# Attention scored two tiles at a time, and a 32 bytes longer mu tile, in a fused local-attention and channel-mix kernel

## The chip, the core and the metric

The kernel runs on one core of one Trainium2 chip. The metric is the device time of one execution in microseconds (us), over several runs; one more execution is recorded by the hardware profiler, and all views of the profile come from that one. The engines have these names: PE does the matmuls (its weight loads are shown apart, as PEld), DVE is the vector engine, ACT the scalar engine, POOL the GpSimd engine, and SP issues the DMAs.

## What is computed

Attention over a short window is followed by a gated channel mix. The inputs are float32; batch 4, 8 heads, 768 tokens, head dimension 64, so d_model is 512, and d_ff is 1024.

```
for each chunk of 32 queries:
    keys = 8 memory keys + 16 tokens to the left + the 32 of the chunk + 8 to the right   # 64
    a = softmax(q_c @ keys.T / 8);  out_c = a @ values
x = the heads of out put side by side                     # (4, 768, 512)
x_prev = x shifted by one token, zero at the start
xk = mu_k * x + (1 - mu_k) * x_prev;   xr = mu_r * x + (1 - mu_r) * x_prev
v = relu(xk @ w_k) ** 2 @ w_v;         r = sigmoid(xr @ w_r)
result = r * v
```

## The kernel before

**Tiles and units.** Tokens come in 24 tiles of 128 (`t`), and two neighbouring tiles make one of 12 units of 256 tokens (`u`). Attention is done by tile, the channel mix by unit.

**Attention of a tile** (`attention`). `f_load` brings queries and windows of keys, 1 MB, into a buffer with the tag `big` (three buffers, shared with the raw weights). The queries lie block-diagonal: a pair of heads shares the 128 partitions, with zeros off the diagonal, so that one matmul over 128 rows gives 64 rows of scores, 32 queries of either head. `f_s` (line 310) makes 16 such matmuls of 64 columns into the PSUM tile `s`. Each float32 matmul is two weight loads and two MATMUL instructions, so 16 of them are 32 MATMULs in the trace. Softmax follows: maximum on DVE (321), subtraction on DVE (325), exponential on ACT (333), sum, an added constant and a reciprocal on DVE (337 to 339), and the multiplication on DVE or POOL (343). `f_t` (349) transposes on PE into `pt`, `f_bd` copies `pt` into a zeroed block tile `aTz` in two halves (215 on ACT, 217 on DVE), `f_a` (368) multiplies by the values into `px`, and `f_x` copies into `xT`, which has one column more than the unit for the token before it.

**Preparation of a unit** (`prep`). `df` is the difference of neighbouring tokens (424), then for r and after it for k: four instructions of mix with mu (432), a rounded high part `xh`, and the remainder `xl` (442).

**Channel mix of a unit** (`channel_mix`). Everything is split into a high and a low part, and each product is three float32r matmuls. `f_gate` gives `pr` (461, 24 matmuls of 512 columns, into one PSUM tile of two banks), `f_sig` its sigmoid over both halves at once (479); `f_s1` gives `ph` (493, four blocks of 24 matmuls of 256 columns), then relu, square, high and low part as `kh` and `kl` (501 to 518); `f_s2` gives `pv` (549, 48 matmuls of 512 columns in four quarters), `f_o` multiplies by the gate (563), `f_st` stores (566).

**Weights.** Each of the ten 1 MB blocks (two of w_r, four of w_k, four of w_v) arrives as raw float64 words and is turned into a high and a low float32r tile by ACT and DVE: 257, 260, 264, then the high part (215 or 217) and the low part (270). All of that lies at the start of the kernel.

**The order.** The instructions are not ordered by a scheduler at run time. `te_order` writes out an order for PE and gives each entry a due time from `PE_COST`; `Plan.dues` passes due times backwards; `Plan.order` then places the operation that can start first by its own cost table, the earlier due time deciding a tie, and picks the engine where there is a choice (`either`). So every engine's queue is fixed when the kernel is built. A `Slot` stands for a buffer, and an operation that needs a new one must wait until the users of an older one are placed. Before the first `ph` block, gaps that the plan sees on PE are filled with `warm` matmuls on zeros (589), as many as fit by its own table. In the order before, t and a of a tile of unit u+2 come in unit u, one tile in the middle of `ph` and one in the middle of `pv`, and s of the next tile right behind a.

**Places in SBUF.** Tiles of the pool `const` are laid out in order of their declaration: identity, mu (32 bytes in each partition), the split weights, `aTz`, a zero tile; the work buffers follow.

Of the kernel before, what the change touches and what calls it, by code (L numbers as in the profile page):

```python
# [40 lines left out]
PE_COST = {"s": 1.05, "t": 0.45, "a": 1.05, "g": BLOCK, "h": BLOCK, "v": BLOCK}  # L41
# [94 lines left out]
def te_order():  # L136

    nu = B * S // UTOK
    seq = LEAD.split()
    seq = [tuple([x[0]] + [int(n) for n in x[1:].split(".")]) for x in seq]  # L140
    for u in range(nu):
        a, b = 2 * u + 4, 2 * u + 5
        g = [("g", u + 1, c) for c in range(QPU)] if u + 1 < nu else []
# [4 lines left out]
    nq = B * NQT  # L148
    seq = [x for x in seq if not (x[0] in "sta" and x[1] >= nq)]
# [9 lines left out]
def local_attention__then__channel_mix(  # L159
# [72 lines left out]
    o_mu = op(("dma", 0.1), lambda: nc.sync.dma_start(mu_sb, mu))  # L232
# [53 lines left out]
    xslot = {}  # L286

    def attention(t):
        b, i = qts[t]
        u, c = t // QPU, t % QPU  # L290

        def f_load():
            a = T["qk", t] = sb("big", [P, QKW], f"qk{t}")
            nc.sync.dma_start(a, qk[b, i])
# [5 lines left out]
        def f_s():  # L300
            s = T["s", t] = ps("s", f"s{t}")
            s4 = s.rearrange("p (m r k) -> p m r k", m=2, r=NPAIR)
            a = T["qk", t]
            nq = NPAIR * NJ * 2 * CHUNK
            q4 = a[:, :nq].rearrange("p (r j q) -> p r j q", r=NPAIR, j=NJ)
            k4 = a[:, nq:].rearrange("p (r j k) -> p r j k", r=NPAIR, j=NJ)
            for r in range(NPAIR):
                for j in range(NJ):
                    o = 64 * (j % 2)
                    nc.tensor.matmul(  # L310
                        s4[o : o + 64, j // 2, r, :], q4[:, r, j, :], k4[:, r, j, :], start=True, stop=True
                    )

        def f_max():
            s = T["s", t].rearrange("p (m r k) -> p m r k", m=2, r=NPAIR)
            if i == 0:
                nc.vector.memset(s[0:64, 0, :, 0:LEFT], NEG)
            if i == NQT - 1:
                nc.vector.memset(s[64:P, 1, :, LEFT + CHUNK : LEFT + CHUNK + RIGHT], NEG)
            mx = T["mx", t] = sb("sm", [P, 2 * NPAIR], f"mx{t}")  # L320
            nc.vector.reduce_max(mx, T["s", t].rearrange("p (g k) -> p g k", k=NK), axis=AX.X)  # L321

        def f_sub():
            e = T["e", t] = sb("e", [P, 2 * NPAIR, NK], f"e{t}")
            nc.vector.tensor_sub(  # L325
                e,
                T["s", t].rearrange("p (g k) -> p g k", k=NK),
                T["mx", t].unsqueeze(2).to_broadcast([P, 2 * NPAIR, NK]),
            )

        def f_exp():
            e = T["e", t]
            nc.scalar.activation(e, e, AF.Exp, scale=SCALE)  # L333

        def f_sum():
            sm = T["sum", t] = sb("sm", [P, 2 * NPAIR], f"sum{t}")
            nc.vector.reduce_sum(sm, T["e", t], axis=AX.X)
            nc.vector.tensor_scalar_add(sm, sm, 1e-9)
            nc.vector.reciprocal(sm, sm)  # L339

        def f_norm(g):
            e = T["e", t]
            g.tensor_mul(e, e, T["sum", t].unsqueeze(2).to_broadcast([P, 2 * NPAIR, NK]))  # L343

        def f_t():
            p = T["pt", t] = ps("tp", f"pt{t}")
            e = T["e", t].rearrange("p (n r) k -> p n (r k)", r=2)
            for n in range(4):
                nc.tensor.transpose(p[:, n * P : (n + 1) * P], e[:, n, :], id_sb)  # L349
# [8 lines left out]
        def f_a():  # L358
            a = aTz[t % bufs["aT"]].rearrange("p (m g c h) s q -> p m g c h (s q)", m=2, g=2, c=2)
# [3 lines left out]
            for m in range(2):  # L363
                for cc in range(2):
                    for g in range(2):
                        for h in range(2):
                            j = 2 * m + cc
                            nc.tensor.matmul(  # L368
                                p3[64 * h : 64 * h + 64, 2 * g : 2 * g + 2, CHUNK * j : CHUNK * j + CHUNK],
                                v[:, g, h, j, :],  # L370
                                a[:, m, g, cc, h, :],
                                start=True,
                                stop=True,
                            )

        def f_x(e):
            if c == 0:
                x = T["xT", u] = sb("xT", [P, KT, 1 + UTOK], f"xT{u}")
                if units[u][1] == 0:
                    nc.gpsimd.memset(x[:, :, 0:1], 0.0)  # L380
                else:
                    nc.gpsimd.tensor_copy(x[:, :, 0:1], T["xT", u - 1][:, :, UTOK : UTOK + 1])
# [6 lines left out]
        qs, vs, s1, s2, s3 = Slot("big"), Slot("vw"), Slot("s"), Slot("tp"), Slot("tp")  # L389
        m1, m2, e = Slot("sm"), Slot("sm"), Slot("e")  # L390
# [3 lines left out]
        ds, dt, da = (due[x, t] for x in "sta")  # L394
        l = op(("dma", 3.0), f_load, new=[qs])
        lv = op(("dma", 1.5), f_loadv, new=[vs])
        o_s = op(("pe", 1.05), f_s, [l, prior.get("s")], new=[s1], use=[qs], due=ds)
        o_m = op(("dve", 0.62), f_max, [o_s], new=[m1], use=[s1], due=ds + 3)
        o_b = op(("dve", 0.62), f_sub, [o_m], new=[e], use=[s1, m1], due=ds + 4)
        o_e = op(("act", 0.55), f_exp, [o_b], use=[e])  # L400
        o_u = op(("dve", 0.98), f_sum, [o_e], new=[m2], use=[e])
        o_n = op(either(dve=(0.62, True), pool=(1.0, True)), f_norm, [o_u], use=[e, m2])
# [4 lines left out]
        prior.update(s=o_s, t=o_t, a=o_a)  # L407
# [3 lines left out]
        xdone[t] = op(either(act=(0.5,), dve=(0.61,)), f_x, deps, new=[xslot[u]] if c == 0 else [], use=[s3, xslot[u]], due=da + 4)  # L411
# [38 lines left out]
    def channel_mix(u):  # L450
        b, t0 = units[u]

        def f_gate(c):
            if c == 0:
                T["pr", u] = ps("g", f"pr{u}", QPU)
            p = T["pr", u][:, c * DM : (c + 1) * DM]
            xh, xl = T["xh", u, 1], T["xl", u, 1]
            wh, wl = ([w[k // 2][:, k % 2 * DM : (k % 2 + 1) * DM] for k in range(KT)] for w in wr_hl)
            for k in range(KT):
                for n, (x, w) in enumerate(((xh, wh[k]), (xh, wl[k]), (xl, wh[k]))):  # L460
                    nc.tensor.matmul(  # L461
                        p, x[:, k, c * P : (c + 1) * P], w, start=(k + n == 0), stop=(k == KT - 1 and n == 2)
                    )

        gs = Slot("g")
        grp = []
        for c in range(QPU):
# [4 lines left out]
                    new=[gs] if c == 0 else [], use=list(mix[u, 1][2:]) + ([gs] if c else []),  # L472
                    due=due["g", u, c],
                )
            )

        def f_sig():
            g = T["sg", u] = sb("sg", [P, QPU * DM], f"sg{u}")
            nc.scalar.activation(g, T["pr", u], AF.Sigmoid)

        sgs = Slot("sg")
        o_g = op(("act", 0.48 * QPU + 2.6), f_sig, grp, new=[sgs], use=[gs], due=due["g", u, 1] + BLOCK + 4)
# [49 lines left out]
        for c in range(QPU):  # L532
# [36 lines left out]
            o_o = op(("dve", 0.62), f_o, [prev, o_g], new=[os], use=[s, sgs], due=dv + BLOCK + 2)  # L569
# [4 lines left out]
    for t in range(len(qts)):  # L574
        attention(t)
# [67 lines left out]
```

## Time and profile before

| what | us |
|---|---|
| median of 3 runs (lowest, highest) | 439.28 (439.17, 439.79) |
| the profiled execution, its own time | 439.1 |
| its span in the profile | 437.3 |
| PE busy, share of the span | 430.8, 99% |
| PE weight loads busy | 382.6, 88% |
| DVE busy | 257.8, 59% |
| ACT busy | 194.2, 44% |
| POOL busy | 26.4, 6% |
| moved by DMA | 55.15 MB |

A row of the groups view reads: line, engine, operation, output and inputs, shapes, number of instructions, then busy time in us and the mean of one in ns, then the idle time of the engine ahead of them with what ended it. The chain of waits is followed back from the last instruction, and each of its rows has a start, a length and what filled it. PE being busy for 99% of the span says little by itself, since the `warm` matmuls count as busy too, and since a matmul is counted from its start to its modelled end, so that neighbours overlap.

### The profile page before, as it was taken

How to read it: one execution, taken by the hardware profiler on the slowest of the kernel's cores; microseconds unless marked ns; L12 is line 12 of the kernel's file. 1: busy time of each engine (PE TensorE's matmuls, PEld its weight loads, DVE VectorE, ACT ScalarE, POOL GpSimd, SP SyncE). 2: the span in 40 equal slices, each digit the busy share in tenths (PEclk: the TensorE clock that was granted, in tenths of full speed). 3: DMA queues.
4: the chain of work that ended last, by engine and by line, in shares of the span. 5: the costliest groups of instructions: out<-in, count | busy, mean ns of one | idle time of the engine just before them, and what ended most of it. 6: DMA issues, size and time to landing. Idle time of an engine off the chain costs nothing.

```text
span 437.3 us, 8807 instructions
## 1 busy us (share of the span) xinstructions
PE 430.8 (99%) x3868; PEld 382.6 (88%) x3868; DVE 257.8 (59%) x426; ACT 194.2 (44%) x266; POOL 26.4 (6%) x33
## 2 busy tenths in 40 slices
PE   9999999989999999999999999999999999999996
PEld 8899988888898898898898898898898898798894
DVE  2899999973654745744844835835736737522121
ACT  1767595552353353264254354354354354152150
POOL 2100030100100100100100100100100010000000
PEclk9999999999999999999999999999999999999999
DMA  8988767621331431421512422413401200000101
GB/s 323 411 318 298 295 247 272 257 93 51 143 130 45 165 105 53 183 68 79 190 54 94 171 69 100 169 43 128 168 28 46 73 25 1 25 25 0 49 0 48
DMA packets 12901, 55.15 MB, mean 126 GB/s; under 512 B 1472, under 2 KB 1600, under 8 KB 9280
## 3 DMA queue, kind: packets, MB, share of 16 engines
q1 hardware_dynamic: 12864, 54.60, 33.8%
q8 instruction: 30, 0.49, 0.5%
q14 instruction: 7, 0.06, 0.0%
HBM read 48.30 MB, written 6.29 MB: 125 GB/s over the span
## 4 chain that ended last, share of the span: by engine, by line
PE 94%; DVE 3%; ACT 2%; issue 0%
PE ph L493 30%; PE pv L549 30%; PE pr L461 15%; PE px L368 6%; PE warm L589 6%; PE s L310 5%; PE pt L349 2%; ACT aTz L215 1%; DVE e L343 1%; DVE o L563 0%; DVE df L432 0%; DVE mx L321 0%; ACT L333 0%; DVE xl L442 0%; DVE mag L264 0%; DVE df L424 0%
## 5 line engine op out<-in xcount | busy, mean ns | idle before, releaser
L493 PE MATMUL ph<-xh,wkh 128*128 128x256 f32 x384 | 109.6, 285 | 0.0
L493 PE MATMUL ph<-xh,wkl 128*128 128x256 f32 x384 | 107.8, 281 | 0.0
L493 PE MATMUL ph<-xl,wkh 128*128 128x256 f32 x384 | 107.8, 281 | 0.0
L549 PE MATMUL pv<-wvh,kh 128*128 128x512 f32 x192 | 77.8, 405 | 0.0
L549 PE MATMUL pv<-wvh,kl 128*128 128x512 f32 x192 | 76.1, 396 | 0.0
L549 PE MATMUL pv<-wvl,kh 128*128 128x512 f32 x192 | 75.6, 394 | 0.0
L493 PEld LDWEIGHTS ph<-xh,wkh 128*128 128x128 f32 x384 | 72.3, 188 | 1.2
L493 PEld LDWEIGHTS ph<-xl,wkh 128*128 128x128 f32 x384 | 72.4, 188 | 0.5
L493 PEld LDWEIGHTS ph<-xh,wkl 128*128 128x128 f32 x384 | 72.4, 188 | 0.0
L518 DVE TENSOR_TENSOR kl<-kf,kh 128x512 fp32r<-128x512 f32 x45 | 31.1, 691 | 69.7 <-ACT kh L215 69.6
L501 ACT ACTIVATE kf<-ph 128x512 f32<-128x512 f32 x48 | 28.7, 598 | 80.5 <-PE ph L493 80.5
L549 PEld LDWEIGHTS pv<-wvh,kl 128*128 128x128 f32 x192 | 36.0, 188 | 8.7
L549 PEld LDWEIGHTS pv<-wvh,kh 128*128 128x128 f32 x192 | 36.1, 188 | 8.4
L549 PEld LDWEIGHTS pv<-wvl,kh 128*128 128x128 f32 x192 | 36.1, 188 | 7.9
L461 PE MATMUL pr<-wrh,xl 128*128 128x512 f32 x96 | 38.1, 397 | 0.0
L461 PE MATMUL pr<-wrh,xh 128*128 128x512 f32 x96 | 38.0, 396 | 0.0
L461 PE MATMUL pr<-wrl,xh 128*128 128x512 f32 x96 | 37.8, 394 | 0.0
L217 DVE COPY aTz<-pt 64x512 f32<-64x512 f32 x29 | 20.0, 690 | 26.4 <-PE pt L349 26.3
L343 POOL TENSOR_TENSOR e<-e,sum 128x512 f32<-128x512 f32 x10 | 16.7, 1667 | 261.0 <-DVE sum L339 261.0
L424 DVE TENSOR_TENSOR df<-xT 128x1024 f32<-128x1024 f32 x12 | 14.7, 1223 | 28.7 <-ACT xT L215 28.7
L333 ACT ACTIVATE e<-e 128x512 f32<-128x512 f32 x24 | 15.2, 632 | 36.3 <-DVE e L325 36.2
L508 ACT ACTIVATE kf<-kf 128x512 f32<-128x512 f32 x48 | 30.3, 631 | 1.2
(55 smaller groups left out, 576.2 us busy)
## 6 DMA issues: line engine op xcount, KB each, us to landing
qk<-in_qk_dram SPq DMA_DIRECT2D x24, 1024.0 KB, 7.4
vw<-in_vw_dram SPq DMA_DIRECT2D x24, 512.0 KB, 3.8
out_dram<-o SPq DMA_DIRECT2D x24, 256.0 KB, 2.0
raw<-in_w_k_dram SPq DMA_DIRECT2D x4, 1024.0 KB, 5.3
raw<-in_w_v_dram SPq DMA_DIRECT2D x4, 1024.0 KB, 8.0
raw<-in_w_r_dram SPq DMA_DIRECT2D x2, 1024.0 KB, 9.8
id_sb<-in_ident_dram SPq DMA_DIRECT2D x1, 64.0 KB, 8.9
mu_sb<-in_mu_dram SPq DMA_DIRECT2D x1, 4.0 KB, 9.4
```

What stands on the lines that cost most here:

```text
L217: e.tensor_copy(dst, src)
L310: nc.tensor.matmul(s4[o : o + 64, j // 2, r, :], q4[:, r, j, :], k4[:, r, j, :], start=True, stop=True)
L333: nc.scalar.activation(e, e, AF.Exp, scale=SCALE)
L343: g.tensor_mul(e, e, T["sum", t].unsqueeze(2).to_broadcast([P, 2 * NPAIR, NK]))
L368: nc.tensor.matmul(p3[64 * h : 64 * h + 64, 2 * g : 2 * g + 2, CHUNK * j : CHUNK * j + CHUNK], v[:, g, h, j, :], a[:, m, g, cc, h, :], sta ...
L461: nc.tensor.matmul(p, x[:, k, c * P : (c + 1) * P], w, start=(k + n == 0), stop=(k == KT - 1 and n == 2))
L493: nc.tensor.matmul(p[:, i * UTOK : (i + 1) * UTOK], w[:, fc], x[:, k], start=(k + n == 0), stop=(k == KT - 1 and n == 2),)
L501: e.activation(r, T["ph", u, f], AF.Relu)
L508: e.activation(q, q, AF.Square)
L518: e.tensor_sub(l, T["kf", u, f], T["kh", u, f].bitcast(F32))
L549: nc.tensor.matmul(p, x[:, tc_], w, start=(f + n == 0), stop=(f == FT - 1 and n == 2))
L589: nc.tensor.matmul(warm[:, :P], zero_sb, zero_sb, start=True, stop=True)
```

## The change

It has two parts.

- Attention goes by units. Queries are no longer block-diagonal: the two heads of a pair lie in partitions 0 to 63 and 64 to 127, and each is multiplied by itself, 64 rows by 32 columns, into a bank of its own. A load is 768 KB in place of 1 MB. The scores of a unit are 64 matmuls (`f_s` in the new `scores`) into one PSUM tile of two banks, and each step of softmax is one instruction over 1024 elements. `f_t`, `f_bd`, `f_a`, `f_x` stay by tile, with other index patterns. The token before a unit is copied on ACT in place of POOL. The gate has its PSUM in two buffers of the tag `m` with a sigmoid for each half. The buffer counts change: `big` 3 to 4, `x4` 5 to 4, `e` 2 to 1 (twice as large), `xT` 3 to 2, `m` 3 to 4, `g` gone, `s` twice as large. The written order changes: both tiles of unit u+1 (no longer of u+2) go through t after the second `ph` block of unit u and through a after the third, s of unit u+2 follows, and the gate of unit u+1 comes after the first quarter of `pv`.
- The tile of mu is declared with 64 bytes in each partition in place of 32, of which half is used, so that all tiles behind it lie 32 bytes further on.

```diff
-LEAD = "s0 t0 a0 s1 t1 a1 s2 t2 a2 s3 g0.0 g0.1 t3 a3 s4"
+LEAD = "s0 t0 t1 a0 a1 s1 g0.0 g0.1"
-QKW = NPAIR * NJ * (2 * CHUNK + NK)
+QKW = NPAIR * NJ * (CHUNK + NK)
-PE_COST = {"s": 1.05, "t": 0.45, "a": 1.05, "g": BLOCK, "h": BLOCK, "v": BLOCK}
+PE_COST = {"s": 1.9, "t": 0.45, "a": 1.05, "g": BLOCK, "h": BLOCK, "v": BLOCK}
...
-        seq += h[:2] + [("t", a)] + h[2:3] + [("a", a), ("s", b)] + h[3:] + g + [("t", b)]
-        seq += v[:1] + [("a", b), ("s", a + 2)] + v[1:]
+        seq += h[:2] + [("t", a), ("t", b)] + h[2:3] + [("a", a), ("a", b), ("s", u + 2)] + h[3:]
+        seq += v[:1] + g + v[1:]
...
-        "big": 3, "vw": 2, "x4": 5,
-        "e": 2, "sm": 2, "xT": 3, "kf": 2, "sg": 2, "o": 3,
-        "s": 1, "tp": 2, "g": 1, "m": 3, "aT": 2,
+        "big": 4, "vw": 2, "x4": 4,
+        "e": 1, "sm": 2, "xT": 2, "kf": 2, "sg": 2, "o": 3,
+        "s": 1, "tp": 2, "m": 4, "aT": 2,
...
-    mu_sb = const.tile([P, 2, KT], F32, tag="mu", name="mu_sb")
+    mu_sb = const.tile([P, 4, KT], F32, tag="mu", name="mu_sb")
...
+    def scores(u):
+        def f_s():
+            s = T["s", u] = ps("s", f"s{u}", QPU)
+            s5 = s.rearrange("p (h c r k) -> p h c r k", h=2, c=QPU, r=NPAIR)
...
+                for r in range(NPAIR):
+                    for j in range(NJ):
+                        for h in range(2):
+                            z = slice(64 * h, 64 * h + 64)
+                            nc.tensor.matmul(
+                                s5[CHUNK * j : CHUNK * (j + 1), h, c, r, :], q4[z, r, j, :], k4[z, r, j, :],
+                                start=True, stop=True,
+                            )
...
+        l = [op(("dma", 2.3), lambda t=t: f_load(t), new=[x]) for t, x in zip(ts, qs)]
+        o_s = op(("pe", 1.9), f_s, l + [prior.get("s")], new=[s1], use=qs, due=ds)
+        o_m = op(("dve", 1.15), f_max, [o_s], new=[m1], use=[s1], due=ds + 4)
+        o_b = op(("dve", 1.15), f_sub, [o_m], new=[e], use=[s1, m1], due=ds + 5.5)
+        o_e = op(("act", 1.0), f_exp, [o_b], use=[e])
+        o_u = op(("dve", 1.55), f_sum, [o_e], new=[m2], use=[e])
+        o_n = op(either(dve=(1.15, True), pool=(2.2, True)), f_norm, [o_u], use=[e, m2])
...
-            if c == 0:
-                T["pr", u] = ps("g", f"pr{u}", QPU)
-            p = T["pr", u][:, c * DM : (c + 1) * DM]
+            p = T["pr", u, c] = ps("m", f"pr{u}_{c}")
...
+        def f_sig(c):
+            if c == 0:
+                T["sg", u] = sb("sg", [P, QPU * DM], f"sg{u}")
+            nc.scalar.activation(T["sg", u][:, c * DM : (c + 1) * DM], T["pr", u, c], AF.Sigmoid)
```

More of the change, by code (lines that the diff above doesn't have):

```diff
@@ L141, in te_order @@
     for u in range(nu):
-        a, b = 2 * u + 4, 2 * u + 5
-        g = [("g", u + 1, c) for c in range(QPU)] if u + 1 < nu else []
+        a, b = 2 * u + 2, 2 * u + 3
+        g = [("g", u + 1, c) for c in range(QPU)]
         h = [("h", u, f) for f in range(FT // 2)]
         v = [("v", u, c, n) for c in range(QPU) for n in range(2)]
-        seq += h[:2] + [("t", a)] + h[2:3] + [("a", a), ("s", b)] + h[3:] + g + [("t", b)]
-        seq += v[:1] + [("a", b), ("s", a + 2)] + v[1:]
-    nq = B * NQT
-    seq = [x for x in seq if not (x[0] in "sta" and x[1] >= nq)]
+        seq += h[:2] + [("t", a), ("t", b)] + h[2:3] + [("a", a), ("a", b), ("s", u + 2)] + h[3:]
+        seq += v[:1] + g + v[1:]
+    last = {"s": nu, "g": nu, "t": B * NQT, "a": B * NQT}
+    seq = [x for x in seq if x[1] < last.get(x[0], nu)]
     due, t = {}, 8.0
@@ L286, in local_attention__then__channel_mix, with f_load, f_max, f_sub @@
     xslot = {}
-    def attention(t):
+    NG = 2 * QPU * NPAIR
+    def scores(u):
+        ts = range(u * QPU, (u + 1) * QPU)
+        def f_load(t):
+            b, i = qts[t]
+            a = T["qk", t] = sb("big", [P, QKW], f"qk{t}")
+            nc.sync.dma_start(a, qk[b, i])
+        def f_s():
+            s = T["s", u] = ps("s", f"s{u}", QPU)
+            s5 = s.rearrange("p (h c r k) -> p h c r k", h=2, c=QPU, r=NPAIR)
+            nq = NPAIR * NJ * CHUNK
+            for c, t in enumerate(ts):
+                a = T["qk", t]
+                q4 = a[:, :nq].rearrange("p (r j q) -> p r j q", r=NPAIR, j=NJ)
+                k4 = a[:, nq:].rearrange("p (r j k) -> p r j k", r=NPAIR, j=NJ)
+                for r in range(NPAIR):
[6 more added lines that the diff above has]
+                            )
+        def f_max():
+            s5 = T["s", u].rearrange("p (h c r k) -> p h c r k", h=2, c=QPU, r=NPAIR)
+            for c, t in enumerate(ts):
+                if qts[t][1] == 0:
+                    nc.vector.memset(s5[0:CHUNK, :, c, :, 0:LEFT], NEG)
+                if qts[t][1] == NQT - 1:
+                    nc.vector.memset(s5[P - CHUNK : P, :, c, :, LEFT + CHUNK : LEFT + CHUNK + RIGHT], NEG)
+            mx = T["mx", u] = sb("sm", [P, NG], f"mx{u}")
+            nc.vector.reduce_max(mx, T["s", u].rearrange("p (g k) -> p g k", k=NK), axis=AX.X)
+        def f_sub():
+            e = T["e", u] = sb("e", [P, NG, NK], f"e{u}")
+            nc.vector.tensor_sub(
+                e,
+                T["s", u].rearrange("p (g k) -> p g k", k=NK),
+                T["mx", u].unsqueeze(2).to_broadcast([P, NG, NK]),
+            )
+        def f_exp():
+            e = T["e", u]
+            nc.scalar.activation(e, e, AF.Exp, scale=SCALE)
+        def f_sum():
+            sm = T["sum", u] = sb("sm", [P, NG], f"sum{u}")
+            nc.vector.reduce_sum(sm, T["e", u], axis=AX.X)
+            nc.vector.tensor_scalar_add(sm, sm, 1e-9)
+            nc.vector.reciprocal(sm, sm)
+        def f_norm(g):
+            e = T["e", u]
+            g.tensor_mul(e, e, T["sum", u].unsqueeze(2).to_broadcast([P, NG, NK]))
+        qs = [Slot("big") for _ in ts]
+        s1, m1, m2, e = Slot("s"), Slot("sm"), Slot("sm"), Slot("e")
+        ds = due["s", u]
+        l = [op(("dma", 2.3), lambda t=t: f_load(t), new=[x]) for t, x in zip(ts, qs)]
[5 more added lines that the diff above has]
+        o_n = op(either(dve=(1.15, True), pool=(2.2, True)), f_norm, [o_u], use=[e, m2])
+        prior.update(s=o_s)
+        return o_n, e
@@ L298, in f_loadv @@
             nc.sync.dma_start(v, vw[b, i])
[L300 to L312, printed above, removed]
@@ L331, in f_exp @@
[L331 to L343, printed above, removed]
         def f_t():
@@ L362, in f_a @@
             p3 = p.rearrange("p (r q) -> p r q", r=NPAIR)
[L363 to L374, printed above, removed]
+            for j in range(NJ):
+                for g in range(2):
+                    for h in range(2):
+                        nc.tensor.matmul(
+                            p3[64 * h : 64 * h + 64, 2 * g : 2 * g + 2, CHUNK * j : CHUNK * j + CHUNK],
+                            v[:, g, h, j, :],
+                            a[:, h, g, j, :],
+                            start=True,
+                            stop=True,
+                        )
         def f_x(e):
@@ L393, in attention @@
             xslot[u] = Slot("xT")
-        ds, dt, da = (due[x, t] for x in "sta")
-        l = op(("dma", 3.0), f_load, new=[qs])
+        dt, da = due["t", t], due["a", t]
         lv = op(("dma", 1.5), f_loadv, new=[vs])
[L397 to L402, printed above, removed]
         o_t = op(("pe", 0.45), f_t, [o_n, o_id, prior.get("t")], new=[s2], use=[e], due=dt)
@@ L463, in f_gate @@
                     )
-        gs = Slot("g")
+        def f_sig(c):
+            if c == 0:
+                T["sg", u] = sb("sg", [P, QPU * DM], f"sg{u}")
+            nc.scalar.activation(T["sg", u][:, c * DM : (c + 1) * DM], T["pr", u, c], AF.Sigmoid)
+        sgs = Slot("sg")
+        gs = [Slot("m") for _ in range(QPU)]
         grp = []
@@ L471, in channel_mix @@
                     grp[-1:] + list(mix[u, 1][:2]) + wdeps(wr_hl, range(KT // 2)),
-                    new=[gs] if c == 0 else [], use=list(mix[u, 1][2:]) + ([gs] if c else []),
-                    due=due["g", u, c],
-                )
-            )
[L477 to L482, printed above, removed]
+                    new=[gs[c]], use=list(mix[u, 1][2:]), due=due["g", u, c],
+                )
+            )
+        o_g = []
+        for c in range(QPU):
+            o_g.append(
+                op(
+                    ("act", 0.5 + 1.3 * (c == 0)), lambda c=c: f_sig(c), grp[c : c + 1] + o_g[-1:],
+                    new=[sgs] if c == 0 else [], use=[gs[c], sgs], due=due["g", u, QPU - 1] + BLOCK + 2,
+                )
+            )
         ks = []
@@ L568, in channel_mix @@
             os = Slot("o")
-            o_o = op(("dve", 0.62), f_o, [prev, o_g], new=[os], use=[s, sgs], due=dv + BLOCK + 2)
+            o_o = op(("dve", 0.62), f_o, [prev, o_g[c]], new=[os], use=[s, sgs], due=dv + BLOCK + 2)
             op(("dma", 0.75), f_st, [o_o], use=[os], due=dv + BLOCK + 6)
@@ L573, in local_attention__then__channel_mix @@
         weight(i)
-    for t in range(len(qts)):
-        attention(t)
+    for u in range(NU):
+        soft = scores(u)
+        for t in range(u * QPU, (u + 1) * QPU):
+            attention(t, *soft)
     for u in range(NU):
```

43 lines of the change are left out of this document (11 added, 32 removed).

## The prediction

> **What bounds the kernel now.** I read the page first, then the chain of waits from the end to the front.
>
> ```profile
> span 437.3 us, 8807 instructions
> PE 430.8 (99%) x3868; PEld 382.6 (88%) x3868; DVE 257.8 (59%) x426; ACT 194.2 (44%) x266; POOL 26.4 (6%) x33
> DVE  2899999973654745744844835835736737522121
> ```
>
> DVE is full only in slices 3 to 8 (22 to 87 us) and mostly at 0.4 to 0.8 later. So two stages have to be told apart. The chain through one unit of the later stage:
>
> ```profile
> 136.05 2.80 PE pv L549 x12
> 138.85 1.08 PE px L368 x32
> 139.93 0.93 PE s L310 x32
> 140.86 8.60 PE pv L549 x36
> 149.46 5.70 PE ph L493 x48
> ...
> 155.59 2.81 PE ph L493 x24
> ...
> 160.43 3.06 PE ph L493 x24
> ```
>
> The pieces left out are PE's too (t, the second a and s, the gate). The next `pv` block begins at 169.51, 33.46 us after the first, and no other engine has a piece between them:
>
> ```profile
> 136.05:169.51 33.46, 33.46 (x305) 29.59 (x305) 19.38 (x34) 14.37 (x21) 1.96 (x2) 1.00 0.32 112
> ```
>
> In this row of the windows view PE (second figure) is busy throughout, DVE for 19.38 and ACT for 14.37 us. Here time is won only by shorter PE work. The end has PE alone as well:
>
> ```profile
> 382.80 11.39 PE ph L493 x96
> 394.19 5.61 PE pr L461 x24
> 399.80 11.20 PE pv L549 x48
> 411.00 11.27 PE ph L493 x96
> 422.26 11.21 PE pv L549 x48
> ```
>
> The last `pv` block ends at 422.26 + 11.21 = 433.47; the 3.8 us to the end of the span are the product, its store and the closing, and the change leaves them. The start is the other stage:
>
> ```profile
> 44.84 2.43 PE warm L589 x20
> 47.27 8.45 PE ph L493 x72
> ```
>
> ```profile
> L589 PE MATMUL warm<-zero_sb 128*128 128x128 f32 x220 | 29.0, 290 | 1.1 <-DVE zero_sb L204 1.1
> ```
>
> Until the first `ph` block at 47.27 us PE is largely on fillers (220 in all), behind it there are none. Between 74 and 92 us the chain runs through DVE and ACT, but PE has other matmuls beside it; the view of waits has only this for PE, at the `px` with which the chain comes back to PE:
>
> ```profile
> PE px L368 <- ACT aTz L215: 1.3, 2, 1.1
> ```
>
> That is 1.3 us in two waits, the longest 1.1.
>
> So the time is the start of the first `ph`, plus the PE work left then, plus a little stall, plus 3.8.
>
> **The scores.** A run of 32 MATMULs took 0.93 us, which is 58 ns for a float32 matmul of two instructions. Before, a unit has 2 x 16 matmuls: 1.87 us. After, it has 64, each with half the rows and half the columns: 128 instructions, 768 MATMULs more in all. No row shows a tile of 64 by 32. If nothing overlaps that does not now, the price is 64 x 58 ns = 3.73 us (1.87 more); if all eight places of the array run beside each other, 16 x 58 ns = 0.93 (0.93 less). Between these ends there are two readings. Matmuls of the two heads follow each other in different row halves; where they run in pairs, it is 32 x 58 ns = 1.87. And the weight loads:
>
> ```profile
> L310 PEld LDWEIGHTS s<-qk 128*64 128x64 f32 x768 | 24.5, 138 | 1.2 <-issue 0.7
> L493 PEld LDWEIGHTS ph<-xh,wkl 128*128 128x128 f32 x384 | 72.4, 188 | 0.0
> ```
>
> Sixty-four columns more cost 50 ns, so 32 fewer are worth some 25 ns of the 58; if the loads set the step, 64 x 33 ns = 2.1 us. The two nearest readings lie at 1.87 and 2.1; I take 1.95, 0.08 more a unit, **+1.0 us** in 12 units, with ends at -11.2 and +22.4.
>
> **Entering and leaving narrow matmuls.** In the quiet unit, three blocks of `ph` take 5.70 + 2.81 + 3.06 = 11.57 against 11.39 undisturbed (382.80), `pv` 2.80 + 8.60 = 11.40 against 11.20, and `px`, which is entered from full-width matmuls, 1.08 against 0.93 for `s`, entered from `px`. That is 0.18 + 0.20 + 2 x 0.15 = 0.68 us a unit for two visits, 0.34 each. The new order has one visit, with both a and s in it: -0.34. But a and s no longer have one tile shape, so a further change comes in between, at the 0.15 of `px`: -0.19 net. Ten units have both visits behind the first `ph`: **-1.9 us**, between 0 and -3.4.
>
> **The start.** DVE sets when the w_k tiles are done; the last three low parts end just as `ph` begins:
>
> ```profile
> 20.53 1.23 DVE L424 TENSOR_TENSOR df<-xT 128x1024 f32<-128x1024 f32 x1
> ...
> 43.33 3.48 DVE L270 TENSOR_TENSOR wkl<-mag,wkh 128x1024 fp32r<-128x1024 f32 x3
> ```
>
> What the change does to DVE ahead of that needs these rows:
>
> ```profile
> L321 DVE TENSOR_REDUCE mx<-s 128x8 f32<-128x512 f32 x24 | 16.4, 684 | 0.5
> L339 DVE RECIPROCAL sum<-sum 128x8 f32<-128x8 f32 x24 | 4.9, 203 | 0.8
> L338 DVE TENSOR_SCALAR sum<-sum 128x8 f32<-128x8 f32 x24 | 4.1, 171 | 0.8
> L442 DVE TENSOR_TENSOR xl<-df,xh 128x1024 fp32r<-128x1024 f32 x12 | 14.6, 1216 | 0.1
> ```
>
> Wide instructions: 1.22 in place of 2 x 0.685 saves 0.15, six times in the two units before `ph`, and the two small ones are paid twice less (2 x 0.37): -1.6 us. Sum, reciprocal and product of the second unit (1.22 + 0.37 + 1.22 = 2.8) now are due only for the t after the second `ph` block, behind the w_k work: up to -2.8. And w_r can be worked earlier:
>
> ```profile
> 0.00:10.00 10.00, 8.95 (x105) 8.53 (x105) 2.23 (x5) 1.91 (x2) 2.28 (x8) 1.00 0.81 315
> 10.00:20.00 10.00, 9.53 (x146) 8.65 (x147) 7.78 (x17) 5.97 (x10) 2.13 (x3) 1.00 1.04 415
> 7.12 3.28 SPq L243 DMA_DIRECT2D raw<-in_w_r_dram  x2
> ```
>
> In these rows of the windows DVE (fourth figure) idles 10.0 of the first 20 us, and the loads of w_r are issued at 7.12 us only, when the first `s` gives back one of three buffers. With four, two of them for queries, both loads go out at once, and 0.5 MB less stands ahead of them; some 2 us of their work can fall into the idle time, 4.3 at most (the two low parts, one join and one shift). Against that, the first unit's softmax is one long chain, and I find its `df` no earlier than 20.5. Together between 0 and -8.7; I take -4.5, about half, since four buffers for `x4` in place of five hold back the high and low parts, and since the fillers are counted from the plan's costs, not from what the chip does. The first `ph` then starts near 42.8.
>
> That moves PE work behind `ph`: two t, two a and one s that came before it, 2 x 0.44 + 3 x 1.08 = 4.1 us. Net **-0.4 us**. The stall behind it stays at the present 1.1, since DVE has about as much to do in the first unit as PE has:
>
> ```profile
> L264 DVE SCALAR_TENSOR_TENSOR mag<-mag,raw 128x1024 uint32<-128x1024 uint32 x10 | 13.1, 1326 | 0.0
> L260 DVE TENSOR_SCALAR raw<-raw 128x1024 uint32<-128x1024 uint32 x10 | 7.5, 754 | 0.3 <-DMA raw<-in_w_v_dram 0.3
> L432 DVE SCALAR_TENSOR_TENSOR xf<-df,mu_sb,xT 128x256 f32<-128x256 f32 x48 | 20.0, 476 | 0.0
> ```
>
> Four w_v blocks at 0.75 + 1.33 + 1.22 are 13.2; a softmax is 4 x 1.22 + 0.37 = 5.3, a preparation 3 x 1.22 + 8 x 0.48 = 7.5, and some 6 for `kl`, copies and products: 32 against 33.
>
> **What is hidden.** The smaller loads (768 KB in place of 1 MB, 24 times), the shorter softmax, a second sigmoid instruction and the copy on ACT lie beside PE in the quiet stage, where DVE is busy for 19.38, ACT for 14.37 of 33.46 and the DMA engines for a 0.32 share, and nothing of theirs ends a wait. Were the cover gone, the second sigmoid and the copy would cost ACT under 0.5 us a unit, and I give them no part.
>
> **The 32 bytes.** Worked out from the tile sizes, the weights now lie at odd multiples of 32 bytes, `xh`, `xl`, `kh`, `kl` at even ones (three `xT` buffers of 4,128 bytes turn it round); after, all are even. So the two kinds can be read against each other: `ph`, streaming from even places, took 11.27 and 11.39 for 96 x 256 columns; `pv`, streaming from odd ones, 11.20 and 11.21 for 48 x 512, as many columns. Even is 0.06 to 0.19 slower there, but its instructions are twice as many. I take nothing; if it were the place, `pv` and `pr` together (1.5 times as many columns) lose 0.09 to 0.29 a unit, 1.1 to 3.4 us; if an even start helps weights as much, the same on the other side.
>
> **The sum.** 437.3 + 1.0 - 1.9 - 0.4 = 436.0 us of span. The profiled execution took 439.1, 1.8 over its span, and the median of the runs is 439.28, 0.2 higher; with 1.8 the forecast is **437.8 us**. What a measurement of this kernel can tell from no change is about 0.2%, 0.9 us.
>
> **The rivals.** The third of them needs two rows more:
>
> ```profile
> L215 ACT CAST xh<-xf 128x1024 fp32r<-128x1024 f32 x11 | 11.5, 1049 | 34.0 <-DVE xf L432 34.0
> L518 DVE TENSOR_TENSOR kl<-kf,kh 128x512 fp32r<-128x512 f32 x45 | 31.1, 691 | 69.7 <-ACT kh L215 69.6
> ```
>
> - *Every score instruction keeps its slot.* Now 0.93 / 32 = 29 ns; 128 of them are 3.72 us a unit, +22.4 in place of +1.0: 459.2. The steps of 29 ns were seen with two column halves in turn, and nothing shows that row halves run beside each other; the halved weight load and separate banks speak against it. It decides from 2.0 us a unit on. Chance 12%. The Trainium skill, TensorEngine Tiling (Array Packing), section Instruction Overhead, warns of this: each matmul has about 60 cycles of overhead, so a factor is not to be taken from a dimension that is small already. By its figure, as an estimate, 128 x 25 ns (at 2.4 GHz) is 3.2 us a unit and the time about 453; no run here shows a slot by itself, and the 29 ns of the trace neither contradict nor prove it.
> - *All eight places run beside each other*: -11.2 in place of +1.0, 425.6. Two places now give 58 ns a matmul, and nothing shows more. 8%.
> - *The gate waits for its preparation* (slower). Attention of unit u+1 now ends in the unit in which its gate is due. From the second a to `xl`: copy 0.69 (as long as `kl`), `df` 1.23, four mixes at 0.48, high part 1.05, `xl` 1.22, together 6.1; the maximum of s (1.22) and a `kl` (0.69) may stand before it on DVE: 8.0. The cover is s, a `ph` block and a quarter of `pv`: 1.95 + 3.06 + 2.80 = 7.8. The plan moves another `pv` quarter forward when it sees this, but its costs run 5 to 10% under the rows (0.61 for the 0.69 copy), so PE may stand 0.2 to 1 us in each of ten units: about +6, 443.8. It decides as soon as the chain is longer than 7.8 and the plan does not see it. 15%.
> - *The start does not move*: w_k still paces at 47.27 and the 4.1 us behind it are paid: +4.5, 442.3. 13%.
> - *The start moves by all of 8.7*: 433.6. 14%.
> - *The places change the matmuls' pace*: about 440. 5%.
>
> **How the numbers follow.** The forecast has 33%, with its own range from 436 to 440. Below 438.4 (faster by over 0.2%) lie 23 of these 33, the eight places, the full start and a part of the pace: 47%. Within 0.2%: 8 of the forecast, and the near edges of pace, gate and start: 13%. Slower: 40%. The range from 431 to 447 leaves out the two ends of the score price, 20%, and takes in the rest.
>
> **What will show it.** The run of 128 `s` matmuls: 1.95 us; 3.7 or 0.9 name a rival. The first `ph` in the chain: 42.8. The quiet unit: 33.46 + 0.08 - 0.19 = 33.35 us, with no piece of DVE or ACT before `pr`. `pv` x48 in the last unit: 11.20. What would make it wrong most: a score price off by a factor, or the gate's wait in every unit.

## The result, and the profile after

The changed kernel takes 432.79 us (median of 4 runs, 432.37 to 433.76). The kernel before took 439.53 on the same chip (4 runs, 439.17 to 440.41). The ratio is 0.9847, with a 95% interval from 0.9824 to 0.9869, so it is 6.7 us faster, and 5.0 us faster than forecast. The profiled execution of the changed kernel took 433.76, with a span of 432.0.

The page of the changed kernel, the lines that were shown of before (the row of q8 gives packets, MB and the share of 16 DMA engines; before it has 30 packets and 0.49 MB):

```profile
span 432.0 us, 10287 instructions
PE 417.8 (97%) x4662; PEld 376.5 (87%) x4662; DVE 245.0 (57%) x348; ACT 209.4 (48%) x294; POOL 4.4 (1%) x13
DVE  2898989377177168168177177177168158255121
...
q8 instruction: 36, 0.59, 0.6%
```

PE has 794 matmul instructions more (4662 for 3868: 768 of the scores, 26 of the fillers) and yet 13 us less of busy time. DVE and ACT have room as before.

The chain of waits of the changed kernel through a quiet unit:

```profile
130.61 5.49 PE pv L567 x24
136.10 5.49 PE pr L473 x24
141.59 5.49 PE pv L567 x24
147.09 5.47 PE ph L511 x48
152.55 0.87 PE pt L373 x8
153.43 2.83 PE ph L511 x24
156.25 2.02 PE px L390 x64
158.27 1.41 PE s L311 x89
159.68 2.94 PE ph L511 x24
```

The next `pv` begins at 162.62, so the unit takes 32.01 us, against 33.46 before and 33.35 forecast. No piece of DVE or ACT stands in it, so the gate does not wait for its preparation. The scores take 1.41 us (the chain steps on 89 of their 128 MATMULs), not 1.95. But the wide matmuls are shorter too, with the same instructions: `pv` 2 x 5.49 = 10.98 for 11.40, `pr` 5.49 for 5.59, `ph` 5.47 + 2.83 + 2.94 = 11.24 for 11.57. In the last unit the last `pv` block of 48 takes 11.02 (11.21 before). Something works on the pace of every wide matmul.

The start in the chain of the changed kernel:

```profile
34.15 1.28 ACT L480
...
36.06 1.28 ACT L336
...
38.43 1.28 ACT L480
39.72 0.01 issue
39.73 0.60 ACT sg L480
40.32 3.16 ACT mag L257 x3
...
47.53 1.15 PE px L390 x32
48.68 8.37 PE ph L511 x72
```

The first `ph` comes at 48.68, not at 42.8; before it came at 47.27. The three rows without a tile name are loads of ACT's function tables, 1.28 us each: sigmoid, exponential, sigmoid again. Only behind them comes `mag` of the raw weights, and behind that the tiles that PE waits for.

The view of waits of the changed kernel (us in total, times, longest):

```profile
PE s L311 <- issue: 4.0, 4, 1.5
PE ph L511 <- issue: 2.1, 2, 1.4
```

Here PE waits for nothing that the profile names, 6.1 us in six pauses. (The expectation of units_split counts each from the start of the instruction ahead of it, which gives 7.5 us.) All six lie inside a run of scores or in the `ph` block behind it; the kernel before has none of them. Two of them in the chain:

```profile
58.14 1.31 PE s L311 x83
59.45 0.97 issue
60.43 0.33 PE s L311 x11
...
93.06 0.56 PE ph L511 x3
93.62 1.43 issue
95.05 2.55 PE ph L511 x21
```

In the trace's DMA records a packet of 16 KB on the instruction queue (q8) starts 1.2 to 1.8 us ahead of each pause: at 58.04, 92.38, 127.36, 285.54, 318.52 and 352.04 us, 0.96 to 1.41 us long. In the four units between, such packets start later in the unit, at 160.12, 192.68, 225.69 and 257.57, within the `ph` block that follows the scores, and there PE does not pause. (The one at 127.36 starts in that block too, and its pause of 0.71 us at 128.93 is one of the shortest.)

Two more facts of the trace tie the pauses to these packets. PE goes on 1.3 to 1.6 us after the end of the packet, in all six. And if all instructions of PE in the trace are counted, weight loads and MATMULs and the 47 others, the pauses stand behind the first 1729, 2497, 3265, 6849, 7617 and 8385 of them: the distances are multiples of 256. That is close to what one packet holds, since 9371 instructions and 36 packets make 260 to a packet (before, 7805 and 30 make 260 too).

So three things stood open: why the wide matmuls are quicker, what the pauses are, and what holds the start.

### The profile page after: what moved, and what is told of

It reads as the page before. It is cut to its first block, busy times and chain, and to the rows that moved or that the text cites. A ratio compares the mean times of both kernels' runs of the same rounds, so it can differ in the third digit from the quotient of the medians.

```text
span 432.0 us, 10287 instructions
## 1 busy us (share of the span) xinstructions
PE 417.8 (97%) x4662; PEld 376.5 (87%) x4662; DVE 245.0 (57%) x348; ACT 209.4 (48%) x294; POOL 4.4 (1%) x13
## 4 chain that ended last, share of the span: by engine, by line
PE 91%; ACT 3%; issue 2%; DVE 2%; DVEq 0%; ACTq 0%
PE ph L511 31%; PE pv L567 31%; PE pr L473 14%; PE px L390 5%; PE s L311 4%; PE warm L609 3%; PE pt L373 2%; ACT mag L257 1%; ACT wkh L215 1%; ACT L480 1%; DVE mag L264 0%; DVE raw L260 0%; DVE xf L446 0%; DVE df L446 0%; ACT L336 0%
## 5 line engine op out<-in xcount | busy, mean ns | idle before, releaser
L567 PE MATMUL pv<-wvh,kh 128*128 128x512 f32 x192 | 74.8, 390 | 0.0
L536 DVE TENSOR_TENSOR kl<-kf,kh 128x512 fp32r<-128x512 f32 x47 | 32.4, 690 | 57.2 <-ACT kh L215 57.0
L581 DVE TENSOR_TENSOR o<-pv,sg 128x512 f32<-128x512 f32 x24 | 16.6, 692 | 70.0 <-PE pv L567 70.0
L609 PE MATMUL warm<-zero_sb 128*128 128x128 f32 x246 | 31.3, 290 | 1.0 <-DVE zero_sb L204 1.0
L609 PEld LDWEIGHTS warm<-zero_sb 128*128 128x128 f32 x246 | 30.4, 205 | 1.4 <-DVE zero_sb L204 1.0
L480 ACT ACTIVATE sg<-pr 128x512 f32<-128x512 f32 x24 | 14.3, 598 | 34.6 <-PE pr L473 34.5
```

The costliest lines, as they stand in the source:

```text
L480: nc.scalar.activation(T["sg", u][:, c * DM : (c + 1) * DM], T["pr", u, c], AF.Sigmoid)
L536: e.tensor_sub(l, T["kf", u, f], T["kh", u, f].bitcast(F32))
L567: nc.tensor.matmul(p, x[:, tc_], w, start=(f + n == 0), stop=(f == FT - 1 and n == 2))
L581: nc.vector.tensor_mul(o, T["pv", u, c], T["sg", u][:, c * DM : (c + 1) * DM])
L609: nc.tensor.matmul(warm[:, :P], zero_sb, zero_sb, start=True, stop=True)
```

## Experiments on the places of the tiles

The theory of the forecast was that places give nothing. Its rivals were that the absolute place (odd or even multiple of 32 bytes) sets the pace, or the relation of the two operands' places. By the addresses in the built programs, the work tiles (`xh`, `xl`, `kh`, `kl`) lie behind the weights at an offset, modulo 2048 bytes, of 672 before and 704 after. The 32 bytes of mu move both kinds of tile and leave the offset alone. What changes it are two other edits: one buffer of `xT` less, 4,128 bytes, takes 32 off modulo 2048, and the two tiles of `sm` (the maxima and sums of softmax), now 64 bytes each in place of 32, add 64.

**units_odd**: the changed kernel without the longer mu tile.

```diff
-    mu_sb = const.tile([P, 4, KT], F32, tag="mu", name="mu_sb")
+    mu_sb = const.tile([P, 2, KT], F32, tag="mu", name="mu_sb")
```

> The changed kernel with the tile of mu as it was before: every split weight, xh, xl, kh and kl then lies at an odd multiple of 32 bytes. If the place of the tiles sets the matmuls' pace (theory place), pv x48 in the last unit goes back from 11.02 to 11.20 us, pr from 5.49 to 5.59, and the time rises by 12 x 0.28 = 3.4 us or more, to 436 to 439. If the pace comes from the new order of work alone (theory order), pv stays at 11.02 and the time within 1 us of 432.8. The run of 128 score matmuls is 1.41 us by both.

Measured: 433.25 (433.04 to 434.01), ratio to before 0.9862 (0.9846 to 0.9877); the change with the 32 bytes had 0.9847 (0.9824 to 0.9869). The 32 bytes of this change are worth 0.5 us at most, and the intervals overlap.

**old_weights_even**: the kernel before with the longer mu tile. **old_all_odd**: the kernel before with 48 bytes more in each `xT` buffer, which puts the offset at 768. **old_all_even**: both.

```diff
-                x = T["xT", u] = sb("xT", [P, KT, 1 + UTOK], f"xT{u}")
+                x = T["xT", u] = sb("xT", [P, KT * (1 + UTOK) + 12], f"xT{u}")[:, : KT * (1 + UTOK)].rearrange("p (k n) -> p k n", k=KT)
```

> The kernel before with the longer mu tile alone: weights at even multiples of 32 bytes; xh, xl, kh, kl, which were even, become odd. By theory place, in the form that the streamed operand counts: pv x48 11.02 and pr 5.49 (both stream weights), ph (streams xh, xl) as slow as before or slower; time 437 or less, 3 us under before. In the form that both operands count, pv gains less. By theory order nothing changes: pv 11.20, 439.5.

> The kernel before with the longer mu tile and 48 bytes more in each xT buffer, so that all tiles from the weights on lie at even multiples of 32 bytes, as in the changed kernel (where one xT buffer is odd). By theory place this has the pace of the changed kernel in the old order: pv x48 11.02, pr 5.49, ph x48 in the quiet unit near 5.47; per unit 0.3 to 0.6 us less, time 433 to 436. By theory order 439.5.

> The kernel before with 48 bytes more in each xT buffer and mu as it was: weights odd as before, xh, xl, kh, kl odd. By theory place, streamed operand: pv 11.20 as before, ph slower than 11.27 to 11.39 for 96, by as much as pv gains from an even place (1.6%, 0.18): time up by 2 us. If the stationary operand counts, pv (kh odd) slows too. By theory order 439.5.

Measured: 439.64, ratio 1.0003 (0.9993 to 1.0013), for the mu tile alone, with the pace of before (`pv` x48 11.20). With offset 768 it is 436.86, ratio 0.9940 (0.9923 to 0.9956), and 437.22, ratio 0.9946 (0.9926 to 0.9965), whether both kinds of tile lie at even or at odd multiples of 32. So it is not the absolute place, and the relation does count.

**units_mixed**, **units_far**, **units_farther**: the changed kernel with a longer zero tile, which lies between the weights and the work buffers. 8, 16 and 32 words more put the offset at 736, 768 and 832.

```diff
-    zero_sb = const.tile([P, P], F32, tag="zero", name="zero_sb")
+    zero_sb = const.tile([P, P + 8], F32, tag="zero", name="zero_sb")[:, :P]
```

> The changed kernel with 32 bytes more in the zero tile, so that the weights stay at even multiples of 32 bytes and xh, xl, kh, kl move to odd ones. The runs so far point to theory relation: the pace hangs on how the places of the two operands of a matmul stand to each other, not on either by itself. Then this goes back to the pace of before: pv x48 in the last unit 11.20 (11.02 now), pr 5.59 (5.49), ph slower in the quiet unit, and the time 3 to 6 us over 432.8. If units gain only by order, it stays within 1 us of 432.8.

> The changed kernel with the work buffers 64 bytes further from the weights (offset 768 in place of 704, both multiples of 64; every place is otherwise as in the changed kernel, and the absolute place of the streamed operand is the one that it has there, plus 64). Theory, that the pace goes by the offset between stationary and streamed operand and that 64 bytes are its period: 432 to 434, within 0.3% of the changed kernel, residual runs of 24 at 5.44 to 5.50, in a shift of twice the bytes that cost 8.5 us in units_mixed. Rival, that 704 is a lucky place and any other costs: 439 to 442, residual runs of 24 at 5.60.

> The changed kernel with the work buffers 128 bytes further from the weights (offset 832). At 704 all wide groups are quick, at 768 the values and the residual are (5.47, 5.44) and the hidden layer is not (5.75 a group of 48 for 5.47). Theory, that odd multiples of 64 are the good ones (period 128): 432 to 434, hidden group of 48 at 5.47. Rival, that the pace has no period that these few places show, and 704 is one good place: 435 to 440, one of the three groups slower than at 704.

Measured: 441.31 (440.45 to 441.83), ratio 1.0035 (1.0022 to 1.0049), at 736; 437.40 (436.46 to 438.36), ratio 0.9954 (0.9936 to 0.9971), at 768; 439.91 (437.88 to 442.48), ratio 1.0017 (0.9995 to 1.0038), at 832. So a zero tile that is 32 bytes longer takes away the whole gain of the change and more. Three pieces of a quiet unit in the chain of units_mixed:

```profile
134.19 5.60 PE pv L567 x24
139.78 5.60 PE pr L473 x24
...
150.99 5.68 PE ph L511 x48
```

The same pieces in the chain of units_far:

```profile
165.98 5.47 PE pv L567 x24
171.44 5.44 PE pr L473 x24
...
182.32 5.75 PE ph L511 x48
```

At 736 all three are slow. At 768 `pv` and `pr` are as quick as at 704 and `ph` is slower than anywhere. At 832, a multiple of 64 too, they take 5.60, 5.60 and 5.66. The kernel before at 768 (old_all_even), brought there by `xT` and not by the zero tile, has nearly the paces of units_far: 5.75 for `ph` x48 and 5.47 for `pr`. So it is the offset that counts and not the tile that was lengthened. My expectation that 64 or 128 bytes are a period therefore fell: 704 is a good place, and which others are is not known from these five.

**old_near**: the kernel before with the zero tile 32 bytes longer and nothing else, so that it has the changed kernel's offset.

> The kernel before with nothing changed but a zero tile that is 32 bytes longer, so that its work buffers lie at offset 704 from the weights, where the changed kernel has them (before: 672; old_all_even and old_all_odd: 768). Theory, that the pace goes by this offset and that at 704 all three kinds of wide group are quick (2 x 2.74, 5.49 and 5.47 + 2.83 + 2.94 us a unit for values, residual and hidden layer, where the kernel before has 11.40, 5.59 and 11.57): a unit shorter by about 0.6 us, the whole by some 7: 431.5 to 433.5, that is, as fast as the changed kernel with 32 bytes alone. Rival, that 704 is quick only in the order by units, and in the old order each multiple of 64 gives what 768 gave: 436 to 438. Rival, that the offset does nothing and the buffers of old_all_even did it: 439 to 440.

Measured: 434.27 (433.47 to 434.51), ratio 0.9871 (0.9855 to 0.9888). Its chain through a quiet unit:

```profile
163.60 5.51 PE pr L461 x24
169.11 0.44 PE pt L349 x4
169.55 2.77 PE pv L549 x12
172.32 1.08 PE px L368 x32
173.40 0.93 PE s L310 x32
174.33 8.46 PE pv L549 x36
182.79 5.46 PE ph L493 x48
188.25 0.44 PE pt L349 x4
188.69 2.83 PE ph L493 x24
191.52 1.08 PE px L368 x32
192.60 0.93 PE s L310 x32
193.53 3.02 PE ph L493 x24
```

The unit is 32.96 us (33.46 before), and `ph`, `pr`, `pv` have nearly the pieces of the changed kernel. This run separates the change into its two parts, medians in us:

| offset | order before | order by units |
|---|---|---|
| 672 | 439.42 | not run |
| 704 | 434.27 | 432.79 |
| 736 | not run | 441.31 |
| 768 | 436.86 | 437.40 |
| 832 | not run | 439.91 |

Of the 6.7 us, 5.2 come with the offset, with no edit of the attention at all. At equal offset the order by units is 1.5 us faster at 704 (1.0 with units_odd, 433.25, whose tiles lie at the very places of old_near) and 0.5 slower at 768, and in both rows the intervals of the ratios overlap. What makes an offset good was not found.

Nor does the offset settle the pace alone. In two units of the changed kernel, with `xh`, `xl`, the weights and even the PSUM banks at the same places, the chain has

```profile
307.96 5.47 PE ph L511 x48
...
374.87 5.66 PE ph L511 x48
```

which is 113 and 118 ns from one MATMUL to the next. The slower pace stands behind the first pause (5.65 at 80.28) and behind the last one (this one, and 11.31 for the 96 of the last unit, where old_near has 10.90), the quicker one in the eight units between. So at 704 both paces occur, while the quiet units at 672, 736, 768 and 832 show only 5.65 to 5.75. What switches between them was not found.

## Experiments on the scores

**units_r_inside**: the changed kernel with the loops of the scores in the order h, j, r. The same 64 matmuls run, but each follows three others into the same place of the array, where the changed kernel goes to another place each time.

```diff
-                for r in range(NPAIR):
-                    for j in range(NJ):
-                        for h in range(2):
+                for h in range(2):
+                    for j in range(NJ):
+                        for r in range(NPAIR):
```

> The changed kernel with the loops of the score matmuls turned round: the four pairs r lie innermost, so four matmuls in a row use the same place of the array, in place of eight different ones. If the 22 ns a matmul (1.41 us for 64) come from places that run beside each other, a matmul costs 58 ns or more now, the run 3.7 us or more, the time 28 us or more over 432.8. If they are a step of issue, of 5.5 ns for each of 256 instructions, whatever the place, the run stays at 1.41 us. All other pieces are unchanged by both.

Measured: 459.87, a single execution, 27.1 us over the changed kernel where 28 or more were expected. The run of scores in its chain:

```profile
167.66 4.36 PE s L311 x128
```

A float32 matmul of 64 by 32 takes 4.36 / 64 = 68 ns when its neighbour uses the same place, and 1.41 / 64 = 22 ns when it uses another. The change of pace is the overlap of places. And the pauses are gone: the view of waits has no row of issue for PE behind the first `ph`. Packets on q8 start inside all ten runs of scores behind it (63.04, 98.67 and so on to 381.32 us). What is missing is not the packet but the haste: 256 instructions, weight loads and MATMULs, go in 4.36 us here and in 1.41 us in the changed kernel, and one packet holds 16 KB and takes about 1 us.

**units_split**: the changed kernel with the scores in two bursts of 32 matmuls, one behind the two t, one behind the two a.

```diff
-        seq += h[:2] + [("t", a), ("t", b)] + h[2:3] + [("a", a), ("a", b), ("s", u + 2)] + h[3:]
+        seq += h[:2] + [("t", a), ("t", b), ("s", u + 2, 0)] + h[2:3] + [("a", a), ("a", b), ("s", u + 2, 1)] + h[3:]
```

> The changed kernel with the scores of a unit in two halves: one tile behind the two t, one behind the two a. Six of the twelve score runs of the changed kernel hold a pause of 0.9 to 1.75 us in them or just behind, 7.5 us together, each beside a 16 KB packet of the instruction queue. Theory fetch: 256 PE instructions in 1.41 us are taken faster than the next 16 KB come, so the pauses go when the burst is halved; the second visit costs up to 0.34 us in ten units; time 4 to 7 us under 432.8, 426 to 429. Rival: the pauses are waits for loads or for a buffer, or come from other DMA traffic; then they stay, and the time is 433 to 436.

Measured: 427.82 (425.65 to 428.74), ratio 0.9723 (0.9692 to 0.9755), 5.0 us under the changed kernel. The view of waits of units_split, the row of the scores, and two of its bursts in the chain:

```profile
PE s L313 <- issue: 0.9, 2, 0.4
```

```profile
182.17 0.79 PE s L313 x53
...
187.90 0.79 PE s L313 x53
```

Instead of 6.1 us of issue there is 0.9 with its scores, half of it ahead of the first `ph`, and none with `ph`. The one behind the first `ph`, 0.4 us at 66.23, has no packet near it (they start at 60.16 and 68.23), so it is not of the kind of the six. The split costs a second visit: 1.58 us for 1.41, and a quiet unit of 32.30 (159.34 to 191.64) for 32.01, some 3 us in ten units. The first `ph` also starts 3.0 us earlier in this kernel's trace (45.60 for 48.61 from the first instruction), since the plan, with other due times, puts no exponential between the two sigmoids. So the pauses go and the start moves, and only the two together are timed here.

That fast bursts outrun the fetching of instructions is thus shown in three ways: the pauses stand at distances of 256 instructions or multiples of it and end 1.3 to 1.6 us after a packet, they go when the burst is slow, and they go when it is halved. How far ahead the queue fetches was not measured.

## Experiments on the start

**units_one_sigmoid**: the changed kernel with both halves of the sigmoid in one step of the plan, so that no exponential can come between them.

```diff
-        def f_sig(c):
-            if c == 0:
-                T["sg", u] = sb("sg", [P, QPU * DM], f"sg{u}")
-            nc.scalar.activation(T["sg", u][:, c * DM : (c + 1) * DM], T["pr", u, c], AF.Sigmoid)
+        def f_sig():
+            T["sg", u] = sb("sg", [P, QPU * DM], f"sg{u}")
+            for c in range(QPU):
+                nc.scalar.activation(T["sg", u][:, c * DM : (c + 1) * DM], T["pr", u, c], AF.Sigmoid)
```

> The changed kernel with both halves of the gate's sigmoid in one step of the plan, so that no exponential comes between them. In the changed kernel the table is loaded three times in a row around 34 to 39 us on ACT, 3.8 us, and the three raw weights behind them wait from 37 to 40.2 and later. Theory ACT: w_k is late by that, and the first ph block starts up to 2.5 us earlier, at 46 to 47; time 430.5 to 432. Rival: DVE or the loads pace the start; then ph stays at 48.4 to 48.7 and the time within 0.5 of 432.8.

Measured: 430.72 (429.95 to 431.70), ratio 0.9791 (0.9770 to 0.9812), 2.1 us under the changed kernel. From its chain:

```profile
38.40 3.15 ACT mag L257 x3
...
46.76 8.36 PE ph L505 x72
```

`mag` begins 1.92 us earlier than in the changed kernel (38.40 for 40.32), and so does the first `ph` (46.76 for 48.68). The table loads are 22 in place of 24. The start was held by ACT, by two table loads of 1.28 us too many.

**units_split_sigmoid**: both edits together.

> The two edits of units_split (427.82 alone, 5.0 us below the changed kernel) and units_one_sigmoid (430.72 alone, 2.1 below) together. Theory: they remove different things, the pauses in the score bursts and the late start of the hidden layer, so they add: 425.5 to 426.5, no pause inside a score run, first hidden-layer matmul by 46.8 us, 11 table loads each way. Rival: the split has moved the start by itself (its first hidden-layer matmul was some 3 us earlier than the changed kernel's), and the sigmoids then add nothing: 427.4 to 428.7.

Measured: 428.03 (426.85 to 430.52), ratio 0.9750 (0.9708 to 0.9792), the same as units_split alone. The rival holds: the split had moved the start already. units_split is the fastest of all that ran.

## Why the prediction was right in sign and off in size

The forecast was 436.0 us of span; it came to 432.0. By its own steps:

- **The scores, +1.0.** The mechanism was right (they overlap, they do not keep a slot), the price was not. The two readings taken were pairs (1.87) and the weight loads' step (2.1). Measured is 1.41, which is 0.45 less a unit than the 1.86 before, so -5.4 by the forecast's own count of 12 units. The row of the weight loads shows why the second reading misled: one load fell from 138 to 105 ns, about as assumed, but loads to different places overlap as well. The rival "every score instruction keeps its slot" put a run at 3.72 us; units_r_inside, where neighbours share a place, has 4.36. That its time, 459.87, is so near the 459.2 worked out for the rival is chance: it has the gain of the offset too, no pauses, and a first `ph` at 53.32 us.
- **Entering and leaving narrow matmuls, -1.9.** Right in mechanism, too small. old_near and the changed kernel have the same offset, and between their units, beside the scores, `pv` falls from 11.23 to 10.98, `px` from 2.16 to 2.02, `ph` from 11.31 to 11.24 and `pr` and `pt` by 0.03: 0.49 a unit, 4.9 in ten units, where 0.19 was forecast. That a visit costs `pv` about this much shows in old_near itself: 11.23 in its quiet units and 10.99 and 11.00 in the last two, where nothing breaks in. The further change of tile shape, put at 0.15, does not show. Not all of it need be a price of entering: `ph` behind the t runs at 118 ns a MATMUL to its end (2.83 for 24), at 113 in the block of 48 ahead, so a visit can also change the pace of what follows.
- **The start, -0.4.** This step failed, by its "I take -4.5, about half". It followed DVE, which ends the w_k tiles, and did not ask what ACT would now do ahead of them. A sigmoid in two halves let the plan put an exponential between them, which the forecast had under "What is hidden" with no part for the start. The first `ph` moved by +1.4 us and not by -4.5. Nor did the work move behind it as stated: of the two t, two a and one s, the chain shows one a (1.08 at 57.06) and scores behind the first `ph`, since the plan placed the others ahead of it. The rival "the start does not move" is the nearer one.
- **What had no term: the pauses.** 6.1 us by the view of waits, where the kernel before has 0.2 of issue at its scores and none at `ph`. The stall kept at 1.1 us, on the other hand, is gone: behind the first `ph` the view of waits has no row of the changed kernel but these.
- **The 32 bytes, 0.** For the 32 bytes themselves that is right: units_odd and old_weights_even differ from their partners by 0.5 and 0.2 us. But the step read `ph` against `pv` by the place of one operand alone and so found at most 1.1 to 3.4 us either way. It had the fact in hand that "three `xT` buffers of 4,128 bytes turn it round", and did not follow it to the relation of the two operands, which gave 5.2 us. The rival for the places, about 440, had the other sign.

Put together: at equal offset the order by units gained 1.5 us, where the three terms gave +1.0 - 1.9 - 0.4 = -1.3. That agreement is luck. Scores and visits gave far more than forecast; the pauses, the start and the `ph` groups of the slower pace took it back. The 5.0 us by which the forecast missed are, in size, the 5.2 of the offset.

## What to carry to other kernels

When a change alters buffer counts or sizes, work out how the places of a matmul's two operands shift against each other, and time the old kernel at the new offset before the gain is credited to the new order: a few unused words in one tile were worth up to 8.5 us here. Many small matmuls are cheapest when neighbours use different places of the array, but in bursts short enough that PE does not run out of fetched instructions. Where one step of ACT is cut in two, look at what function the plan can put between the halves.

## What the runs showed of the hardware

- **The pace of a wide matmul depends on the offset between its two operands in SBUF, and not on it alone.** In quiet units groups of 24 with 512 columns took 5.44 to 5.60 us and groups of 48 with 256 columns 5.46 to 5.75, with the same instructions, at five offsets; the two kinds do not have the same good offsets. At 704 both kinds also occur at a second, slower pace (5.60 in one unit of units_odd and three of units_one_sigmoid, 5.66 in the changed kernel).
- **Small tiles at different places overlap threefold:** 22 ns a float32 matmul against 68. The Trainium skill, TensorEngine Tiling (Array Packing), section Key Properties, says that different tiles can load weights and multiply in parallel, and the two orders of the loops agree with it. The Trainium skill, TensorEngine Tiling (Array Packing), section Instruction Overhead, puts about 60 cycles on each matmul, from which the prediction had estimated 3.2 us a unit; the 1.41 us measured are under half of that.
- **PE can outrun its instruction fetch.** The Trainium skill, Runtime: NRT & Kernel Launch, section Instruction fetch mechanics, gives blocks of 16 KiB or 256 instructions, fetched while the block before is executed and mostly hidden. The 36 packets of 16 KB here, and pauses at distances that are multiples of 256 instructions, agree with the size. They were not hidden where 256 instructions were issued in 1.41 us: six pauses, 6.1 us. In units_odd, units_mixed, units_far, units_farther and units_one_sigmoid, which have the same burst, every pause of PE of over 0.3 us behind the first `ph` stands at such a place too.
- **A longer pause goes with a lower granted clock.** In the chain of the changed kernel the pause at 93.62 us lasts 1.43 us, and the clock stays at 1.00. In units_far it lasts longer, and the windows view has a lower clock (the third figure from the end, ahead of the DMA share and GB/s) in that stretch only, 0.50 for 3.4 us:

```profile
93.92 2.36 issue
```

```profile
48.00:100.00 52.00, 48.86 (x649) 45.14 (x645) 39.72 (x55) 28.02 (x41) 1.83 (x2) 0.97 0.51 185
95.76:99.17 3.41, 2.90 (x14) 2.89 (x14) 3.41 (x7) 0.00 (x0) 0.00 (x0) 0.50 0.97 395
100.00:160.00 60.00, 59.13 (x542) 52.84 (x542) 27.98 (x39) 29.12 (x41) 0.00 (x0) 1.00 0.17 63
```

  Half of 3.4 us, 1.7 us, is the most that it can cost. units_mixed and units_farther have the same 0.97 between 48 and 100 us, with pauses of 2.3 and 2.1 us by their views of waits; units_one_sigmoid, with 1.8 us, does not have it. In the single executions of units_far three with a mean clock of 0.996 took 437.9 to 438.4 us and three with 0.998 to 1.0 took 436.5 to 436.9, so the 0.5 us by which it is behind old_all_even may be this. It is also a part of what units_mixed and units_farther lose beyond their units (0.64 x 10 = 6.4 of 8.5 us in units_mixed). That the pause lowers the clock is argued from these traces and was not tried by itself; nor was why the pause is longer in three of them.
